# TensorE issues in written order until attention ends; thresholds move from ScalarE to VectorE

## The chip, the cores and the metric

The kernel runs on one core of a Trainium2 chip. The metric is the device time of one execution in microseconds (us). A core has five engines that run side by side, each working through its own queue in the order fixed when the program is built: TensorE (PE in the profile; its weight loads are PEld), VectorE (DVE), ScalarE (ACT), GpSimd (POOL) and SyncE (SP), which here issues the DMAs. An instruction that waits for another engine holds up all that stands behind it in its queue.

## What is computed

Attention with a threshold, then two feed-forward blocks, for 4 batches of 576 tokens with 8 heads of 64:

```python
scores = scale * np.matmul(q, k.transpose(0, 1, 3, 2))
thresh = np.max(scores, axis=-1, keepdims=True) - tau
scores = np.where(scores >= thresh, scores, -1000000000.0)
scores = scores - np.max(scores, axis=-1, keepdims=True)
attn = np.exp(scores)
attn = attn / (np.sum(attn, axis=-1, keepdims=True) + 1e-09)
x = np.matmul(attn, v)          # then heads side by side: 2304 x 512
...
h = (x @ w1) * (x @ w2) @ w3    # 1024 wide
x = h @ w_out                   # 2304 x 512
...
h = x @ w_in                    # 2048 wide
return np.maximum(0.01 * h, h) @ w_out2
```

## The kernel before, in words

**Steps and units.** Two heads (a pair) are worked on together. The 576 query rows of a pair are cut into group 0 (rows 0 to 255) and group 1 (rows 256 to 575). A pair and a group make a *unit* (32 units); per batch the four units of group 0 come first and then the four of group 1. A unit of group 0 has two *steps*, each with 128 rows of both heads (a double step); a unit of group 1 has one step in which the last 64 rows of both heads share one tile (c is None; a single step) and then two double steps. That gives 80 steps (`STEPS`, L33); the main loop (L450) goes over them.

**One step.** `scores` (L210) computes the scores of the next step n+1 on PE into the PSUM tile `sc`, of which there is one only, so that the scores of step n+1 wait for the mask of step n. Then, for each head, VectorE takes the negated maximum (L232), ScalarE makes the threshold from it (L233) and the exponential (L234). `mask` (L239) at the start of step n multiplies the exponential by "score is at or over the threshold" and sums it, on VectorE (L248). `transposes` (L254) turns the masked tile on PE, five 128 x 128 blocks per head, into `tp` (one buffer) and `tq`; ScalarE and VectorE copy them to `HH` and `tl` (L270 to L284). One step after the last of a unit, `weighted` (L288) computes v^T e on PE (L298, 20 matmul instructions) with a copy on ScalarE; two steps after it, `normalise` (L321) brings the reciprocals of the sums across with 2 to 4 PE instructions (L326, L328), multiplies by them on VectorE and splits the result in two parts on ScalarE and GpSimd.

**Filler.** Between these, PE does feed-forward work, the *filler*: for each batch and group, once its four units are normalised, the generator `gated` (L372) yields 24 pieces of 12 matmuls: 16 pieces psab (L385; products with w1 and w2, two per tile of w12) and 8 pieces psh (L404; the product with the folded weight w3 w_out). Filler made of group 0 runs beside the units of group 1 (256 columns per matmul), filler made of group 1 beside the next group 0 (320 columns). At each step `rate` times the weight of the step (1 or 2) pieces are due, half of them written ahead of the transposes and half behind (L462 to L465). In the first batch the folded weight itself is computed on PE instead (`fold_weights`, L357; L365, 8 blocks of 16 instructions). Filler, fold, v^T e and reciprocals share two PSUM buffers (`ps_w`, tag `w`).

**Weights.** They arrive as 64-bit words and are decoded in halves (`stream`, L108): two ScalarE passes (L150, L152), a shift on VectorE (L153), and an addition on GpSimd (L156); for the w12 and later weights a cast on ScalarE (L158), an addition on GpSimd (L159) and a subtraction on GpSimd or VectorE by turns (L161). `load_halves` (L431) is called at the end of each step; 24 halves serve the folding, 16 more the filler's w12.

**What sets the order.** A scheduler orders each engine's queue when the program is built, by a model of the timing and by priority, which falls in the order of writing. `ahead_of(60)` raises the priority of the scores' matmuls by 60 places, `ahead_of(20)` that of the transposes and of the late items (v^T e, normalising). SP alone keeps the written order (`manual_schedule`, L421) until the first batch's group 1 is through, and the decoding's ScalarE passes keep theirs. After attention (L499) the rest of the filler runs, and then the last feed-forward block (`up`, `down`).

Of the kernel before, what the change touches and what calls it, by code (L numbers as in the profile page):

```python
# [17 lines left out]
P = 128  # L18
# [21 lines left out]
def attention_gated_ffn(ctx: ExitStack, tc: tile.TileContext, qkv, tau, w3t, wout, w12, w2, out):  # L40
# [10 lines left out]

    @contextmanager
    def ahead_of(count):

        before = tc.cur_priority
        tc.cur_priority = start = before - count
        yield
        tc.cur_priority = before + (tc.cur_priority - start)
# [151 lines left out]
    def scores(n):  # L210
# [6 lines left out]
        with ahead_of(60):  # L217
            for half in range(2):
                ks = slice(half * HS, half * HS + HS)
                for a in heads:  # L220
                    if c is None:
                        nc.tensor.matmul(sc[:, a, half, :HS], qz[u % 2], qk[:, ks], start=True, stop=True)  # L222
                    else:
                        r = slice(a * D, a * D + D)
                        o = S + Q0[c] - GROUPS[g][0]
                        nc.tensor.matmul(sc[:, a, half, :HS], qk[r, o:o + P], qk[r, ks], start=True, stop=True)  # L226
        e = apool.tile([P, 2, S], F32, tag="e", name="e", bufs=2)
        ths = []
        for a in heads:
            nm = apool.tile([P, 1], F32, tag="nm", name="nm", bufs=4)  # L230
            th = apool.tile([P, 1], F32, tag="th", name="th", bufs=4)
            nc.vector.tensor_reduce(out=nm, in_=sc[:, a, :, :HS], op=ALU.max, axis=AX.XY, negate=True)  # L232
            nc.scalar.activation(th, nm, AF.Identity, bias=cb, scale=-1.0)  # L233
            nc.scalar.activation(  # L234
                e[:, a].rearrange("p (a b) -> p a b", a=2), sc[:, a, :, :HS], AF.Exp, bias=nm)
            ths.append(th)
# [17 lines left out]
    def transposes(n):  # L254
# [10 lines left out]
        if c is None:  # L265
            tp = ps_a.tile([P, 4, P], F32, tag="tp", name="tp")
            for kc in range(4):
# [4 lines left out]
                tail[D:, :, :D], tq[D:, 0].rearrange("p (a w) -> p a w", a=2))  # L272
            return
# [10 lines left out]
        nc.scalar.copy(tail[D:, :, o:o + P], tq[D:])  # L284
# [72 lines left out]
    def fold_weights():  # L357

        for i in range(KF):
# [4 lines left out]
            for j in range(KF):  # L364
                nc.tensor.matmul(  # L365
                    ps, w3_t[i][:, j * P:j * P + P], wo_t[j // 2][:, (j % 2) * 512:(j % 2) * 512 + 512],
                    start=(j == 0), stop=(j == KF - 1))
            nc.scalar.copy(wt[:, 0, i % 2], ps)
# [50 lines left out]

    in_order = ExitStack()  # L420
# [8 lines left out]
    halves_in = [0]  # L429

    def load_halves(k):  # L431
        for _ in range(k):
            if next(loads, 0) != 0:
                halves_in[0] += 1
                if 10 <= halves_in[0] <= 24 and halves_in[0] % 2 == 0:
                    next(folding)
# [5 lines left out]

    folding = fold_weights()
    scores(0)
    late = {}
    halves = 0.0
    filler = iter(())
    queue = []
    rate, due = 2.0, 0.0
    for n in range(NS):  # L450
        pair, g, c = STEPS[n]
        u = units.index((pair, g))
        weight = 1 if c is None else 2
        mask(n)
        if STEPS[(n + 1) % NS][:2] != (pair, g):
# [6 lines left out]
        run(filler, k // 2)  # L462
        with ahead_of(20):
            transposes(n)
        run(filler, k - k // 2)  # L465
        if STEPS[(n + 1) % NS][:2] != (pair, g):
            late.setdefault(n + 1, []).append(lambda pair=pair, g=g: weighted(pair, g))
            reciprocals(pair, g)
            late.setdefault(n + 2, []).append(lambda pair=pair, g=g: normalise(pair, g))
            if pair % 4 == 3:  # L470
                queue.append((n + 2, pair // 4, g))
        with ahead_of(20):
            for item in late.pop(n, []):
                item()
        if n == 0 or STEPS[n - 1][:2] != (pair, g):
            load_unit(u + 2)
        halves += 1.2 * weight
        load_halves(int(halves))
        halves -= int(halves)
        if queue and queue[0][0] == n:  # L480
            _, b, gg = queue.pop(0)
            while halves_in[0] < 24:
                load_halves(1)
            for _ in filler:
# [11 lines left out]
    for n in sorted(late):  # L496
        for item in late[n]:
            item()
# [138 lines left out]
```

## Time and profile before

| | us |
|---|---|
| Time, median of 3 runs | 1186.98 |
| lowest and highest of the runs | 1185.36, 1188.83 |
| the profiled execution's own time | 1189.11 |
| its span, first to last instruction | 1187.3 |
| mean granted TensorE clock, share of full speed | 0.968 |

The profile is of a single execution. Busy time of an engine counts the union of its instructions; matmuls are pipelined, so one of them is listed longer than the distance to the next start. The granted clock is a share of 2.4 GHz; its levels are 1.2 and 2.4 GHz.

### The profile page before, as it was taken

To read this page: it belongs to the slowest core of one execution; us is meant where nothing else is said; L and a number is where in the kernel's file an instruction comes from. 1 tells how busy PE (TensorE), PEld (TensorE's weight loads), DVE (VectorE), ACT (ScalarE), POOL (GpSimd) and SP (SyncE) were. 2 spreads that over 40 slices of the span, in tenths; PEclk is the share of its full clock that TensorE was granted. 3 is DMA by queue.
4 is the path that set the end of the run, shared out by engine and by line. 5 is a ranking of instruction groups with operands and counts; after the bars stand their busy time and mean duration, and the time that the engine had idled before them with its cause. 6 is when DMAs were issued, how large, how long until landed. Compare 5 with 4: busy or idle time off the path is not lost.

```text
span 1187.3 us, 16135 instructions
## 1 busy us (share of the span) xinstructions
PE 1099.6 (93%) x6288; PEld 864.6 (73%) x6288; DVE 471.5 (40%) x911; ACT 503.7 (42%) x1035; POOL 262.3 (22%) x288
## 2 busy tenths in 40 slices
PE   4799888999979998889998887999999999999998
PEld 2344466888857887667886665986788888888887
DVE  4554556444444544444544353336521121111111
ACT  4654666444443544334443344337732222222232
POOL 2322465111111111110210113547730010000000
PEclk9899989999989999889999888999999999999999
DMA  8542235211111112102111002226520010010000
GB/s 267 180 142 89 87 107 151 59 55 49 39 41 44 53 39 62 30 26 70 38 55 38 12 1 97 82 94 200 173 71 1 1 63 1 1 45 1 1 36 18
DMA packets 35099, 77.58 MB, mean 65 GB/s; under 512 B 4560, under 2 KB 19408, under 8 KB 32976
## 3 DMA queue, kind: packets, MB, share of 16 engines
q1 hardware_dynamic: 34880, 76.56, 20.6%
q8 instruction: 49, 0.80, 0.3%
q14 instruction: 26, 0.21, 0.1%
q10 hardware_dynamic: 144, 0.00, 0.0%
HBM read 67.11 MB, written 9.44 MB: 64 GB/s over the span
## 4 chain that ended last, share of the span: by engine, by line
PE 80%; ACT 8%; DVE 5%; issue 3%; DMA 2%; POOL 2%; SPq 0%; ACTq 0%; DVEq 0%; POOLq 0%
PE psab L385 17%; PE ps L552 15%; PE po L574 15%; PE psh L404 8%; PE av L298 7%; PE sc L226 6%; PE tp L278 5%; PE ps L365 3%; ACT e L234 2%; PE sc L222 2%; DVE nm L232 2%; ACT t L150 1%; DVE t L153 1%; ACT lw L152 1%; DVE e L248 1%
## 5 line engine op out<-in xcount | busy, mean ns | idle before, releaser
L385 PE MATMUL psab<-x,w 128*128 128x256 f32 (+1 forms) x1536 | 240.4, 308 | 10.0 <-ACT w L158 3.6
L385 PEld LDWEIGHTS psab<-x,w 128*128 128x128 f32 x1536 | 215.6, 195 | 33.9 <-issue 14.0
L552 PE MATMUL ps<-h,w 128*128 128x512 f32 (+1 forms) x960 | 215.7, 370 | 1.5 <-ACT w L158 1.2
L574 PE MATMUL po<-w,gg 128*128 128x512 f32 x864 | 213.6, 392 | 1.8 <-ACT gg L559 1.8
L552 PEld LDWEIGHTS ps<-h,w 128*128 128x128 f32 x960 | 169.0, 188 | 37.2 <-ACT w L158 2.5
L574 PEld LDWEIGHTS po<-w,gg 128*128 128x128 f32 x864 | 159.3, 188 | 37.8 <-ACT gg L559 3.0
L232 DVE TENSOR_REDUCE nm<-sc 128x1 f32<-128x576 f32 x144 | 108.8, 756 | 195.6 <-PE sc L226 135.3
L560 DVE TENSOR_TENSOR gg<-gf,gg 128x512 fp32r<-128x512 f32 (+1 forms) x80 | 61.2, 764 | 269.4 <-ACT gg L559 267.8
L557 ACT ACTIVATE gf<-ps 128x512 f32<-128x512 f32 (+1 forms) x80 | 44.2, 554 | 226.5 <-PE ps L552 226.5
L278 PE MATMUL tp<-ident,e 128*128 128x128 f32 x512 | 89.0, 301 | 53.7 <-DVE e L248 49.0
L248 DVE SCALAR_TENSOR_TENSOR e<-sc,th,e 128x576 f32<-128x576 f32 x144 | 112.5, 815 | 56.3 <-ACT e L234 56.0
L278 PEld LDWEIGHTS tp<-ident,e 128*128 128x128 f32 x512 | 64.8, 153 | 72.7 <-issue 57.8
L404 PE MATMUL psh<-gt,w 128*128 128x256 f32 (+1 forms) x768 | 112.8, 301 | 0.5 <-ACT xs L301 0.5
L404 PEld LDWEIGHTS psh<-gt,w 128*128 128x128 f32 x768 | 104.2, 190 | 4.1 <-issue 1.9
L234 ACT ACTIVATE e<-sc,nm 128x576 f32<-128x576 f32 x144 | 105.4, 732 | 1.0
L396 POOL TENSOR_TENSOR gt<-at,gt 128x256 fp32r<-128x256 f32 (+1 forms) x64 | 52.4, 819 | 189.8 <-ACT gt L395 189.8
L226 PE MATMUL sc<-qk 64*128 64x288 f32 x512 | 85.4, 448 | 6.4 <-DVE qk L201 6.0
L233 ACT ACTIVATE th<-nm,cb 128x1 f32<-128x1 f32 x144 | 42.4, 295 | 99.0 <-DVE nm L232 98.9
L298 PE MATMUL av<-HH,vv 128*64 128x256 f32 (+1 forms) x512 | 72.5, 424 | 0.1
L159 POOL TENSOR_TENSOR lw<-t,lw 128x512 int32<-128x512 int32 x48 | 64.8, 1356 | 27.6 <-ACT lw L152 15.8
L226 PEld LDWEIGHTS sc<-qk 64*128 64x128 f32 x512 | 46.5, 194 | 28.8 <-issue 12.3
L153 DVE TENSOR_SCALAR t<-t 128x512 int32<-128x512 int32 x72 | 50.0, 697 | 39.7 <-ACT t L150 39.4
(70 smaller groups left out, 968.3 us busy)
## 6 DMA issues: line engine op xcount, KB each, us to landing
st<-in_w SPq DMA_DIRECT2D x40, 512.0 KB, 4.5
vv<-in_qkv SPq DMA_DIRECT2D x64, 160.0 KB, 2.3
raw<-in_w3t SPq DMA_DIRECT2D x8, 1024.0 KB, 6.9
qk<-in_qkv SPq DMA_DIRECT2D x32, 208.0 KB, 3.6
qk<-in_qkv SPq DMA_DIRECT2D x32, 144.0 KB, 2.9
out<-os SPq DMA_DIRECT2D x18, 256.0 KB, 2.2
raw<-in_wout SPq DMA_DIRECT2D x4, 1024.0 KB, 10.3
raw<-in_w SPq DMA_DIRECT2D x4, 1024.0 KB, 7.3
```

What stands on the lines that cost most here:

```text
L153: nc.vector.tensor_scalar(out=t, in0=t, scalar1=3, scalar2=None, op0=ALU.logical_shift_left)
L159: nc.gpsimd.tensor_tensor(out=lw, in0=t, in1=lw, op=ALU.add)
L226: nc.tensor.matmul(sc[:, a, half, :HS], qk[r, o:o + P], qk[r, ks], start=True, stop=True)
L232: nc.vector.tensor_reduce(out=nm, in_=sc[:, a, :, :HS], op=ALU.max, axis=AX.XY, negate=True)
L234: nc.scalar.activation(e[:, a].rearrange("p (a b) -> p a b", a=2), sc[:, a, :, :HS], AF.Exp, bias=nm)
L248: nc.vector.scalar_tensor_tensor(out=ev, in0=sc[:, a, :, :HS], scalar=th, in1=ev, op0=ALU.is_ge, op1=ALU.mult, accum_out=stat[key][:, o:o ...
L278: nc.tensor.transpose(tp[:, kc], e[:, a, kc * P:kc * P + P], ident)
L298: nc.tensor.matmul(av[a * D:a * D + D, :gw], vv[:, a, kc], rhs, start=(i == 0), stop=(i == NK - 1))
L385: nc.tensor.matmul(ps[:, :gw], w12_t[i][:, a, mat * 512 + kk * P:mat * 512 + kk * P + P], xt[kk][:, c, :gw], start=(m == 0), stop=(m == 11))
L404: nc.tensor.matmul(ps[:, :gw], w34_t[i // 2][:, a, i % 2, o * P:o * P + P], gt[i][:, c, :gw], start=(m == 0), stop=(m == 23))
L552: nc.tensor.matmul(ps[:, :tw], w2_t[j][:, a, kk * P:kk * P + P], h3_t[ci][:, c, kk, :tw], start=(m == 0), stop=(m == 11))
L574: nc.tensor.matmul(po_t[t], gg[:, c, t * P:t * P + P], w2_t[j][:, a, 512:], start=(j == 0 and (a, c) == PASSES[0]), stop=(j == KF2 - 1 and ...
```

## The change

- PE keeps the written order from the start to the end of attention; the priorities (`ahead_of`) are gone.
- The written order of a step is new: scores of the next step; a third of the filler due; v^T e of the previous unit, if due; the transposes of the first head; another third; the transposes of the second head; the reciprocals of the unit before, if due; the last third. Where there is one piece it goes to the first place, two go to the first and second.
- The fold is cut into 16 pieces of 8 matmul instructions. Each of the three filler places takes one, provided that the halves it needs had been decoded before the step began; what is left is written when the first filler is made.
- Half of a step's decoding is written after the first third of filler, the rest at the end, now behind the loads of the unit after next.
- The threshold is made by a VectorE instruction in place of one on ScalarE.

```diff
--- before.py
+++ after.py
...
     def f(ap):
         return ap.bitcast(F32)
-
-    @contextmanager
-    def ahead_of(count):
-
-        before = tc.cur_priority
-        tc.cur_priority = start = before - count
-        yield
-        tc.cur_priority = before + (tc.cur_priority - start)
...
         heads = range(1 if c is None else 2)
         sc = ps_a.tile([P, 2, 2, 512], F32, tag="sc", name="sc")
-        with ahead_of(60):
-            for half in range(2):
...
+        for half in range(2):
+            ks = slice(half * HS, half * HS + HS)
...
             th = apool.tile([P, 1], F32, tag="th", name="th", bufs=4)
             nc.vector.tensor_reduce(out=nm, in_=sc[:, a, :, :HS], op=ALU.max, axis=AX.XY, negate=True)
-            nc.scalar.activation(th, nm, AF.Identity, bias=cb, scale=-1.0)
+            nc.vector.tensor_scalar(out=th, in0=nm, scalar1=-1.0, scalar2=cb, op0=ALU.mult, op1=ALU.add)
             nc.scalar.activation(
                 e[:, a].rearrange("p (a b) -> p a b", a=2), sc[:, a, :, :HS], AF.Exp, bias=nm)
             ths.append(th)
@@ -270,6 +261,7 @@
             nc.scalar.copy(HH[:, :, :, :D], tp.rearrange("p k (a w) -> p k a w", a=2))
             nc.vector.tensor_copy(
                 tail[D:, :, :D], tq[D:, 0].rearrange("p (a w) -> p a w", a=2))
+            yield
             return
         o = Q0[c] - GROUPS[g][0]
         for a in range(2):
@@ -281,7 +273,9 @@
             else:
                 nc.scalar.copy(HH[:, :, a, o:o + P], tp)
             nc.tensor.transpose(tq[:, a], e[:, a, S - P:], ident)
-        nc.scalar.copy(tail[D:, :, o:o + P], tq[D:])
+            if a:
+                nc.scalar.copy(tail[D:, :, o:o + P], tq[D:])
+            yield
 
     xs_t, x_t, rb_t = {}, {}, {}
 
@@ -365,6 +359,8 @@
                 nc.tensor.matmul(
                     ps, w3_t[i][:, j * P:j * P + P], wo_t[j // 2][:, (j % 2) * 512:(j % 2) * 512 + 512],
                     start=(j == 0), stop=(j == KF - 1))
+                if j == 3:
+                    yield
             nc.scalar.copy(wt[:, 0, i % 2], ps)
             nc.vector.tensor_tensor(out=wt[:, 1, i % 2], in0=ps, in1=f(wt[:, 0, i % 2]), op=ALU.subtract)
             yield
@@ -417,6 +413,8 @@
             yield from gn
 
 
+    pe_order = ExitStack()
+    pe_order.enter_context(tc.manual_schedule(engines={mybir.EngineType.PE}))
     in_order = ExitStack()
     in_order.enter_context(tc.manual_schedule(engines={mybir.EngineType.SP}))
     load_tau()
@@ -427,60 +425,83 @@
     issue()
     scale_unit(0)
     halves_in = [0]
+    folded = [0]
 
     def load_halves(k):
         for _ in range(k):
             if next(loads, 0) != 0:
                 halves_in[0] += 1
-                if 10 <= halves_in[0] <= 24 and halves_in[0] % 2 == 0:
-                    next(folding)
 
     def run(gen, k):
         for _ in range(k):
             if next(gen, 0) == 0:
                 return
 
+    def fold_some(most, halves):
+
+        while most and folded[0] < 2 * KF and 8 + 2 * (folded[0] // 2) + 2 <= halves:
+            next(folding, 0)
+            folded[0] += 1
+            most -= 1
+
     folding = fold_weights()
     scores(0)
-    late = {}
-    halves = 0.0
+    weigh, norm = [], []
+    due_halves = 0.0
     filler = iter(())
     queue = []
-    rate, due = 2.0, 0.0
+    rate, due = 0.0, 0.0
     for n in range(NS):
         pair, g, c = STEPS[n]
         u = units.index((pair, g))
         weight = 1 if c is None else 2
+        last_of_unit = STEPS[(n + 1) % NS][:2] != (pair, g)
+        decoded = halves_in[0]
         mask(n)
-        if STEPS[(n + 1) % NS][:2] != (pair, g):
+        if last_of_unit:
             scale_unit(u + 1)
         if n + 1 < NS:
             scores(n + 1)
         due += rate * weight
         k = int(due)
         due -= k
-        run(filler, k // 2)
-        with ahead_of(20):
-            transposes(n)
-        run(filler, k - k // 2)
-        if STEPS[(n + 1) % NS][:2] != (pair, g):
-            late.setdefault(n + 1, []).append(lambda pair=pair, g=g: weighted(pair, g))
+        parts = [(k + 2) // 3, (k + 1) // 3, k // 3]
+        due_halves += 1.2 * weight
+        kh = int(due_halves)
+        due_halves -= kh
+
+        def fill(i):
+            run(filler, parts[i])
+            fold_some(1, decoded)
+
+        fill(0)
+        load_halves(kh // 2)
+        if weigh:
+            weighted(*weigh.pop())
+        pieces = transposes(n)
+        next(pieces)
+        fill(1)
+        for _ in pieces:
+            pass
+        if norm:
+            normalise(*norm.pop())
+        if last_of_unit:
             reciprocals(pair, g)
-            late.setdefault(n + 2, []).append(lambda pair=pair, g=g: normalise(pair, g))
-            if pair % 4 == 3:
-                queue.append((n + 2, pair // 4, g))
-        with ahead_of(20):
-            for item in late.pop(n, []):
-                item()
+            weigh.append((pair, g))
+        elif u and STEPS[n - 1][:2] != (pair, g):
+            norm.append(units[u - 1])
+        fill(2)
         if n == 0 or STEPS[n - 1][:2] != (pair, g):
             load_unit(u + 2)
-        halves += 1.2 * weight
-        load_halves(int(halves))
-        halves -= int(halves)
+        load_halves(kh - kh // 2)
+        if last_of_unit and pair % 4 == 3:
+            queue.append((n + 2, pair // 4, g))
         if queue and queue[0][0] == n:
             _, b, gg = queue.pop(0)
-            while halves_in[0] < 24:
+            while halves_in[0] < 26:
                 load_halves(1)
+            fold_some(2 * KF, 24)
+            next(folding, 0)
             for _ in filler:
                 pass
             if (b, gg) == (0, 0):
@@ -493,9 +514,10 @@
                 in_order.close()
             filler = gated(b, gg)
             rate, due = (1.22, 1.55)[gg], 0.0
-    for n in sorted(late):
-        for item in late[n]:
-            item()
+    weighted(*weigh.pop())
+    run(filler, 2)
+    normalise(B * 4 - 1, 1)
+    pe_order.close()
     s_att.close()
 
 
```

## Rows read from the trace of the kernel before

**Rows 1.** The page, part 1: busy us, share of the span, instructions of each engine
```profile
PE 1099.6 (93%) x6288; PEld 864.6 (73%) x6288; DVE 471.5 (40%) x911; ACT 503.7 (42%) x1035; POOL 262.3 (22%) x288
```

**Rows 2.** Busy time by stretch: us, PE, PEld, DVE, ACT, POOL busy (instructions), PEclk, DMA share, GB/s
```profile
0.00:60.20 60.20, 35.45 (x162) 19.99 (x162) 32.96 (x74) 31.14 (x61) 16.20 (x20) 0.94 0.68 220
60.20:132.00 71.80, 65.77 (x250) 32.52 (x250) 35.67 (x72) 36.32 (x73) 22.09 (x24) 1.00 0.30 96
132.00:227.20 95.20, 85.00 (x540) 63.23 (x538) 54.53 (x109) 59.52 (x126) 44.11 (x46) 0.93 0.40 121
227.20:300.60 73.40, 72.52 (x509) 61.26 (x507) 35.02 (x75) 31.97 (x73) 12.92 (x18) 1.00 0.17 51
300.60:396.90 96.30, 88.22 (x622) 70.59 (x621) 46.84 (x103) 42.81 (x97) 16.17 (x28) 0.95 0.15 44
470.40:566.70 96.30, 84.03 (x577) 65.17 (x576) 46.30 (x101) 41.14 (x92) 14.75 (x26) 0.93 0.15 42
639.90:735.00 95.10, 78.69 (x502) 58.75 (x501) 39.85 (x86) 38.04 (x84) 16.51 (x27) 0.86 0.06 17
```

**Rows 3.** Groups by line, PE, 0 to 745 us: busy us, mean ns, idle before, releasers
```profile
L278 PE MATMUL tp<-ident,e 128*128 128x128 f32 x512 | 89.0, 301 | 53.7 <-DVE e L248 49.0 <-ACT HH L282 3.7 <-ACT HH L270 0.8
...
L365 PE MATMUL ps<-wo,w 128*128 128x512 f32 x128 | 58.5, 601 | 6.3 <-POOL w L156 6.2
```

**Rows 4.** Timeline of all engines, 684.7 to 697.3: start us, us, instructions [idle before, releaser]
```profile
685.65 4.57 PE L385 MATMUL psab<-x,w 128*128 128x256 f32 x36 [0.18 <-DVE xs L329]
...
688.00 0.81 DVE L248 SCALAR_TENSOR_TENSOR e<-sc,th,e 128x576 f32<-128x576 f32 x1
...
690.06 0.60 PE L278 MATMUL tp<-ident,e 128*128 128x128 f32 x4
...
690.70 1.24 PE L226 MATMUL sc<-qk 64*128 64x288 f32 x8
...
691.99 0.76 DVE L232 TENSOR_REDUCE nm<-sc 128x1 f32<-128x576 f32 x1 [2.67 <-PE sc L226]
...
692.78 0.29 ACT L233 ACTIVATE th<-nm,cb 128x1 f32<-128x1 f32 x1 [0.17 <-DVE nm L232]
693.09 0.74 ACT L234 ACTIVATE e<-sc,nm 128x576 f32<-128x576 f32 x1
693.86 0.76 DVE L232 TENSOR_REDUCE nm<-sc 128x1 f32<-128x576 f32 x1 [0.49 <-ACT e L234]
...
694.85 0.72 ACT L234 ACTIVATE e<-sc,nm 128x576 f32<-128x576 f32 x1
695.61 0.82 DVE L248 SCALAR_TENSOR_TENSOR e<-sc,th,e 128x576 f32<-128x576 f32 x1 [0.99 <-ACT e L234]
...
696.58 1.09 PE L278 MATMUL tp<-ident,e 128*128 128x128 f32 x4 [3.95 <-DVE e L248]
```

**Rows 5.** Timeline of PE, 676 to 706
```profile
677.79 2.37 PE L298 MATMUL av<-HH,vv 128*64 128x320 f32 x16
680.10 1.69 PE L385 MATMUL psab<-x,w 128*128 128x256 f32 x12
681.72 1.24 PE L226 MATMUL sc<-qk 64*128 64x288 f32 x8
```

**Rows 6.** Single source lines: count, ns min/median/max, first and last start
```profile
L309 DVE TENSOR_SCALAR rr<-stat x32: 156/161/1256, 24.0 to 721.0; 128x4 f32<-128x4 f32 x16, 128x5 f32<-128x5 f32 x16
...
L153 DVE TENSOR_SCALAR t<-t x72: 409/471/2622, 18.2 to 862.0; 128x512 int32<-128x512 int32 x72
...
L152 ACT ACTIVATE lw<-st x40: 643/663/695, 171.6 to 861.9; 128x512 int32<-128x512 uint32 x40
...
L158 ACT CAST w<-t x48: 600/619/646, 133.1 to 862.5; 128x512 fp32r<-128x512 f32 x48
...
L161 POOL TENSOR_TENSOR w<-lw,w x24: 1268/1357/1738, 134.2 to 862.2; 128x512 fp32r<-128x512 f32 x24
```

**Rows 7.** The page, part 6, DMA issues: count, KB each, median us to landing
```profile
qk<-in_qkv SPq DMA_DIRECT2D x32, 208.0 KB, 3.6
```

More of the change, by code (lines that the diff above doesn't have):

```diff
@@ L1 @@
-from contextlib import ExitStack, contextmanager
+from contextlib import ExitStack
 import concourse.bass as bass
@@ L216, in scores @@
         sc = ps_a.tile([P, 2, 2, 512], F32, tag="sc", name="sc")
-        with ahead_of(60):
-            for half in range(2):
[L219 to L226, printed above, removed]
+        for half in range(2):
+            ks = slice(half * HS, half * HS + HS)
+            for a in heads:
+                if c is None:
+                    nc.tensor.matmul(sc[:, a, half, :HS], qz[u % 2], qk[:, ks], start=True, stop=True)
+                else:
+                    r = slice(a * D, a * D + D)
+                    o = S + Q0[c] - GROUPS[g][0]
+                    nc.tensor.matmul(sc[:, a, half, :HS], qk[r, o:o + P], qk[r, ks], start=True, stop=True)
         e = apool.tile([P, 2, S], F32, tag="e", name="e", bufs=2)
```

## The prediction

> **What bounds it now.** I read the page's busy line first. TensorE (PE) is busy for 1099.6 of 1187.3 us [rows 1], no other engine for half of the span, so the time can only fall where PE stands still or runs slowly. Second, the table of stretches [rows 2], cut where the kind of filler changes: PE's idle time there is length minus PE busy. The stretch 227.2 to 300.6, in which units of group 0 run, is idle for 0.9 us of 73.4: nothing is to be had there, nor in the two later stretches of its kind. The three stretches of group 1 (from 300.6, 470.4 and 639.9) are idle for 8.1, 12.3 and 16.4 us, and their granted clock is 0.95, 0.93 and 0.86. Since the clock has two levels, 1.2 and 2.4 GHz, a share of 2 x (1 - mean) was at the lower one: 10, 13 and 27 us. In the first batch (three stretches up to 227.2) PE idles 24.8, 6.0 and 10.2 us.
>
> Third, the groups by line with what ended the idle time before them: of PE's idle time up to 740 us, 49.0 us is transposes (L278) waiting for the mask (L248) [rows 3]. Fourth, the timeline of one such wait [rows 4]. PE runs 36 psab matmuls in one go until 690.1 while the mask that the next scores need had ended at 688.8 (second mask row: 688.00 + 0.81); the scores start at 690.70. From there VectorE and ScalarE work strictly in turn: maximum 691.99, exp 693.09, maximum 693.86, exp 694.85, then two masks of 0.8 us from 695.61, the last of which ends near 697.2. PE has used up its filler and stands for 3.95 us; the four transposes after it take 1.09 us where they took 0.60 at 690.06, so the lower clock is paid as well. The work is there, but it is done at the wrong moment. What is late is not an engine but the scores, behind filler.
>
> **The change, part by part.**
>
> 1. *Written order on PE, group 1.* A unit has three steps (one single, two double). Its PE work, from starts in one undisturbed part [rows 5]: a piece of 12 psab or psh matmuls 1.6 us (680.10 to 681.72), double scores 1.2 us, v^T e 2.3 us for 16 matmuls (677.79 to 680.10), so 2.9 us for its 20. Five transposes are 0.64 us (690.06 to 690.70, [rows 4]), single scores 1.1 and the reciprocals' four matmuls 0.5 us, as much as four transposes. One unit: 2 x 1.2 + 1.1 + 6.1 x 1.6 + 5 x 0.64 + 2.9 + 0.5 = 20 us; four units 80 us, against 96.3 us per stretch. The idle time and the slow clock account for this: idle 8.1 + 12.3 + 16.4 = 36.8 us, and at the lower clock about 50 us, of which some 7 us are idle inside it; busy time at half clock gives back half, 21 us. Together 58 us to be had at most.
>
> What does written order leave of it? I walk one unit. The wait is now at the scores, for the mask of the step before; behind it on PE's queue stand filler, v^T e and the transposes, all of it. The chain from the end of double scores to the end of the second mask was 691.9 to 697.2 = 5.3 us [rows 4]; with part 2 it is 4.8 us, for a single step about 2.6. Cover between two scores: after the single step's scores one piece and five plus five transposes, with a piece between: 1.6 + 0.64 + 1.6 + 0.64 = 4.5 us over 2.6, no wait. After the first double scores one piece, v^T e and five transposes: 1.6 + 2.9 + 0.6 = 5.1 us over 4.8: it just fits, and any copy that gets between (0.4 to 0.7 us on either engine) shows. After the second, three pieces, ten transposes and 0.5: 6.6 us over 4.8. I charge 0.7 us for the middle one and 0.5 us for filler that waits for one of the two PSUM buffers which filler, v^T e and reciprocals share: the piece behind the reciprocals' matmuls has only 0.64 + 0.5 us for its buffer's evacuation. 1.2 us x 12 units = 14 us; bounds 0 and 12 x 4 = 48 us (as much as now is lost).
>
> 2. *Thresholds on VectorE.* Removes 144 activations of 0.29 us from ScalarE, where each stood ahead of the exp (692.78 ahead of 693.09, [rows 4]). Adds 144 small operations to VectorE; the nearest row, the small tensor_scalar of L309, has a median of 161 ns and would run beside the exp (0.74 us), since the next maximum starts only when that exp has ended. So 0.2 to 0.3 us off the chain, twice per double step. Where PE is the bound this is worth nothing; where nothing covers the chain (the first five steps) 5 x 0.4 = 2 us. The cost could show if the small operation grows: L309 has one case of 1256 ns, and the tensor_scalar of L153 goes from 409 to 2622 ns (both [rows 6]). I take 161 ns as the median and no cost.
> The Trainium skill ("SBUF — State Buffer", Who interferes with whom) says that VectorE's tensor_scalar may need a port pair that GpSimd holds for a whole instruction, the later one being blocked. By that rule a threshold that meets a GpSimd addition of 1.3 us ends up to 0.7 us after the exp; with GpSimd busy for 46% of the third stretch [rows 2] and 36 thresholds in the first batch, 36 x 0.46 x 0.35 on average, the sum would be about 6 us worse. The spread of L153 agrees with the rule; no run here shows it for so small an operand.
>
> 3. *First batch, folding (L365).* Now cut into 16 pieces of 8 matmuls (58.5 us in all, 3.7 us each [rows 3]) and one per filler place, held until the decoded halves stand one step back. Nothing of it comes before step 5, so two pieces that now run before 58 us are left for later: their cover for the first steps is lost, 7 us worse (bounds 4 and 7.4). The 6.2 us of waits for decoded weights (same row) have better lead, but the queue is now blocked behind them: no change, bounds -4 and +6.
>
> 4. *First batch, gated filler (132 to 227.2).* To be had: 10.2 + 6.0 us idle and half of 13 us at the lower clock, 22 us. The filler's weights are decoded just ahead of use, and one half takes ScalarE two passes of 0.66 (L152, and L150 like it) and one of 0.62 (L158), VectorE 0.47 (L153), GpSimd 1.36 and for every other half as much again (L161, and L159 like it) [rows 6]: about 5 us end to end, each pass behind the other engines' other work. In written order scores, v^T e and transposes behind such a piece wait too. ScalarE is the fullest here (59.5 of 95.2 us); squeezed into 80 us of PE work it is at 74%. I charge 10 us for 16 tiles; bounds 0 and 16 x 3.9 = 62 (the whole 5.1 us less the 1.2 us of scores ahead of it).
>
> 5. *Group 0 in later batches.* 12 units; the stretch from 227.2 spends 73.4 us on its eight steps [rows 2], 9.2 us each, so some 8 us of cover stand over 4.8: no wait at the scores. The buffer after the reciprocals' matmuls can cost 0.25 us: 3 us.
>
> 6. *What is moved.* v^T e now goes ahead of the transposes instead of behind the last filler; the reciprocals' matmuls behind them, with their VectorE, ScalarE and GpSimd successors; nothing waits on these for a step. Half of the decoding (with the SP loads that each half issues) moves ahead of the next unit's q, k and v loads on SP. Those are asked for two units (some 20 us) ahead, so I cost it at nothing; without that cover it would be the 3.6 us of one such load [rows 7] per unit. The part behind 735 us keeps its 452 us.
>
> **Sum.** Gain 58 + 22 + 2 = 82; losses 14 + 7 + 10 + 3 = 34 plus 2 us at the end of attention, where no scores are left to overlap. Net 46 us. The profiled execution took 1189.1 us (span 1187.3), 2.1 us over the median of the runs; I take the 46 us off the median: 1141.
>
> **Rivals.**
> - *The wait moves from transposes to scores.* If copies or products that VectorE and ScalarE take in between lengthen the chain from 4.8 to 6.5 us or more, every group 1 unit loses about 1.3 us at the first and some at the second cover, and with the buffers 2.5 to 3 us. For: [rows 4] shows strict turns with no slack. Against: group 0 stretches do not wait at all. 12 x 1.5 more, and a third of that again in the first batch: some 25 us less gain, 1166.
> - *Nearly all is got back.* If the charges of parts 1, 4 and 5 (27 us) mostly do not arise, 1115.
> - *Slower: decoded weights block the queue.* Place: the first 192 psab matmuls. Today PE's order, although fixed, has other work ahead of late weights (6.2 us of waits at L365 in all). If each of the 16 tiles waits the whole 3.9 us, 62 us instead of 10; added stalls at the folding and the lower clock after each wait of this length take the rest. It decides from (46 + 10) / 16 = 3.5 us per tile with every other gain as above, and from 1.9 us if the first rival holds as well. Alone it gives 1193, with the clock about 1205. Against: halves are decoded a step's filler ahead, so half of the tiles have a lead.
> - *The order hardly differs.* PE's queue was already near written order, and times stay at 1187. Against: 36 psab matmuls in one go.
>
> **Chances.** Forecast 0.48, first rival 0.22, all got back 0.10, slower 0.13, no change 0.07. A change under 0.3% (3.6 us) can't be told from none here. Faster 0.80, same 0.07, slower 0.13. The forecast's own range is 1120 to 1158 (half to double its charges); with the first rival's upper end and most of the second it is 1116 to 1184.
>
> **What would show it.** Right: PE's wait for L248 at transposes gone and at the scores (L222, L226) under 15 us in all; idle time in the group 1 stretches under 5 us each and the clock at 1.00 from 230 us on; attention ending near 690 us; exp starting within 0.1 us of the maximum. Wrong: waits at the scores of 1 us and more in each unit (first rival); waits of psab for L158 or L161 above 25 us, with the clock below 0.9 before 230 us (slower); small VectorE rows for the threshold of 0.5 us and more on the chain.

## Result, and the profile after

The changed kernel takes 1118.0 us (median of 4 runs, 1116.9 to 1118.6), the kernel before 1187.9 beside it: a ratio of 0.941, interval 0.939 to 0.943. It is faster by 70 us where 46 were forecast; 1118.0 lies at the lower end of the range, 1116 to 1184, and just below the narrower range that the prediction gave for its own forecast, 1120 to 1158.

Part 1 of the page, to be set beside [rows 1]:

```profile
PE 1062.5 (95%) x6288; PEld 856.3 (77%) x6288; DVE 499.6 (45%) x1055; ACT 475.2 (43%) x891; POOL 262.6 (24%) x288
```

The same 6288 matmuls; TensorE idles for 1116.2 - 1062.5 = 53.7 us of its span instead of 87.7, and is busy for 37 us less. Part of this is the clock: the mean granted clock rose from 0.968 to 0.989, so by 2 x (1 - mean) the time at 1.2 GHz fell from about 76 to 25 us. If work takes twice as long there (four transposes took 1.09 us against 0.60 [rows 4]), this explains at most half of the 51 us, 26 of the 37; the rest stays open. 34 us less idle and 37 us less busy are the 71 us of the span.

The table of stretches of the changed kernel, cut at the same steps as [rows 2] (length, PE, PEld, DVE, ACT, POOL busy with instructions, PEclk, DMA share, GB/s):

```profile
0.00:58.00 58.00, 34.61 (x163) 20.27 (x164) 37.82 (x95) 30.87 (x53) 16.72 (x20) 0.91 0.72 229
58.00:125.30 67.30, 66.16 (x234) 32.35 (x233) 32.28 (x67) 32.43 (x58) 25.89 (x27) 1.00 0.38 124
125.30:212.10 86.80, 75.99 (x540) 61.22 (x539) 61.45 (x132) 56.75 (x107) 39.83 (x42) 0.96 0.34 106
212.10:282.70 70.60, 68.28 (x480) 57.76 (x479) 37.43 (x89) 28.71 (x56) 12.96 (x18) 0.98 0.22 60
282.70:364.50 81.80, 80.54 (x608) 67.10 (x607) 50.42 (x123) 36.98 (x72) 14.24 (x26) 1.00 0.19 55
364.50:435.00 70.50, 68.18 (x478) 58.12 (x477) 37.39 (x89) 28.81 (x56) 12.95 (x18) 0.98 0.16 43
435.00:517.20 82.20, 80.64 (x610) 67.15 (x609) 50.42 (x123) 36.98 (x72) 14.23 (x26) 1.00 0.18 54
517.20:586.20 69.00, 66.68 (x480) 56.71 (x479) 37.39 (x89) 28.69 (x56) 12.97 (x18) 1.00 0.15 44
586.20:665.00 78.80, 77.30 (x584) 64.77 (x584) 42.51 (x103) 33.76 (x68) 14.41 (x27) 1.00 0.07 23
```

The group 1 stretches took 96.3, 96.3 and 95.1 us and take 81.8, 82.2 and 78.8 now: 45 us. Their idle time is 1.3, 1.6 and 1.5 us, their clock 1.00. Up to the change of filler (132.0, now 125.3) 6.7 us went, in the rest of the first batch 95.2 - 86.8 = 8.4. The three group 0 stretches give the other 10 us, but these are lent: some 30 filler matmuls in each (480 instructions against 509 in the first) are left to the stretch behind, about 4 us each at 1.6 us for 12 [rows 5], 12 us in all. The group 1 stretches do that work too: they hold 101 matmuls more than before (608 + 610 + 584 against 622 + 577 + 502), and are shorter by 45 us all the same.

The chain of waits of TensorE, 0 to 680 us (engine, tile and line, what it waited for: us in total, times, longest):

```profile
PE sc L217 <- DVE e L239: 20.0, 11, 4.9
PE sc L217 <- DVE qk L193: 8.3, 2, 6.0
PE tp L270 <- ACT HH L274: 7.3, 10, 1.6
PE sc L213 <- POOL qz L197: 5.8, 8, 2.1
PE psab L381 <- POOL w L153: 1.8, 3, 0.8
```

The 49.0 us in which transposes waited for the mask [rows 3] are gone. Scores wait for it instead, 20.0 us in all, of which 10.0 lie in the first 58 us, where there is no filler.

A unit of group 1 in the timeline of the changed kernel, to be set beside [rows 4] (start, length, instruction, [idle before it]):

```profile
606.03 0.81 DVE L239 SCALAR_TENSOR_TENSOR e<-sc,th,e 128x576 f32<-128x576 f32 x1
...
607.20 1.24 PE L217 MATMUL sc<-qk 64*128 64x288 f32 x8
...
608.49 0.76 DVE L223 TENSOR_REDUCE nm<-sc 128x1 f32<-128x576 f32 x1 [0.89 <-PE sc L217]
609.28 0.74 ACT L225 ACTIVATE e<-sc,nm 128x576 f32<-128x576 f32 x1 [1.44 <-DVE nm L223]
609.28 0.21 DVE L224 TENSOR_SCALAR th<-nm,cb 128x1 f32<-128x1 f32 x1
...
610.15 0.42 DVE L389 TENSOR_TENSOR at<-psab,at 128x256 f32<-128x256 f32 x1 [0.66 <-PE psab L381]
...
610.50 0.75 DVE L223 TENSOR_REDUCE nm<-sc 128x1 f32<-128x576 f32 x1
...
611.32 0.75 ACT L225 ACTIVATE e<-sc,nm 128x576 f32<-128x576 f32 x1
...
612.10 0.82 DVE L239 SCALAR_TENSOR_TENSOR e<-sc,th,e 128x576 f32<-128x576 f32 x1 [0.61 <-ACT e L225]
...
612.73 1.67 PE L381 MATMUL psab<-x,w 128*128 128x256 f32 x12
...
612.85 0.81 DVE L239 SCALAR_TENSOR_TENSOR e<-sc,th,e 128x576 f32<-128x576 f32 x1
...
613.58 0.38 DVE L193 TENSOR_SCALAR qk<-qk,scl 128x320 f32<-128x320 f32 x1
613.88 0.68 DVE L272 COPY HH<-tp 128x512 f32<-128x512 f32 x1
614.03 0.52 POOL L197 COPY qz<-qk 64x64 f32<-64x64 f32 x2 [1.79 <-DVE qk L193]
...
614.61 1.24 PE L213 MATMUL sc<-qk,qz 128*128 128x288 f32 x4 [0.21 <-POOL qz L197]
```

Read it as a race. From the end of the double scores (608.44) the chain goes maximum, exp, a product of the filler, maximum, exp, two masks, the scaling of the next unit's queries and the copies that place them: ready at 614.55, after 6.1 us. TensorE's cover ends with the last piece of filler at 614.40, after 6.0 us. They are level, and TensorE stands for 0.21 us. The profile of before does not show that they are level, since the wait stood elsewhere, though the scaling's length can be read there (0.37 us, the median of its L201). A race that is level means that anything which lengthens the chain shows in full.

### The profile page after: what moved, and what is told of

Read it like the earlier page. It is cut to its first block, busy times and chain, and to the rows that moved or that the text cites. A ratio compares the mean times of both kernels' runs of the same rounds, so it can differ in the third digit from the quotient of the medians.

```text
span 1116.2 us, 16066 instructions
## 1 busy us (share of the span) xinstructions
PE 1062.5 (95%) x6288; PEld 856.3 (77%) x6288; DVE 499.6 (45%) x1055; ACT 475.2 (43%) x891; POOL 262.6 (24%) x288
## 4 chain that ended last, share of the span: by engine, by line
PE 77%; issue 8%; ACT 5%; DVE 4%; POOL 2%; DMA 2%; SPq 0%; ACTq 0%; DVEq 0%; POOLq 0%
PE po L596 16%; PE ps L574 16%; PE psab L381 14%; PE psh L400 9%; PE av L292 6%; PE sc L217 6%; PE ps L359 5%; PE tp L270 4%; PE sc L213 2%; DVE e L239 2%; ACT t L142 1%; DMA st<-in_w 1%; ACT e L225 1%; POOL gt L392 1%; ACT lw L144 1%
## 5 line engine op out<-in xcount | busy, mean ns | idle before, releaser
L400 PE MATMUL psh<-gt,w 128*128 128x256 f32 (+1 forms) x768 | 115.2, 301 | 0.6 <-ACT ht L407 0.5
L217 PE MATMUL sc<-qk 64*128 64x288 f32 x512 | 85.3, 454 | 28.4 <-DVE e L239 20.0
L270 PE MATMUL tp<-ident,e 128*128 128x128 f32 x512 | 80.1, 280 | 7.3 <-ACT HH L274 7.3
L270 PEld LDWEIGHTS tp<-ident,e 128*128 128x128 f32 x512 | 60.6, 143 | 21.7 <-issue 11.6
L151 POOL TENSOR_TENSOR lw<-t,lw 128x512 int32<-128x512 int32 x48 | 64.9, 1357 | 39.4 <-ACT lw L144 24.5
L292 PE MATMUL av<-HH,vv 128*64 128x256 f32 (+1 forms) x512 | 69.5, 415 | 0.0
L551 POOL TENSOR_TENSOR h<-hr,h 128x1024 fp32r<-128x1024 f32 (+1 forms) x10 | 23.8, 2381 | 188.1 <-DVE h L550 188.1
```

What stands on the lines that cost most here:

```text
L151: nc.gpsimd.tensor_tensor(out=lw, in0=t, in1=lw, op=ALU.add)
L270: nc.tensor.transpose(tp[:, kc], e[:, a, kc * P:kc * P + P], ident)
L292: nc.tensor.matmul(av[a * D:a * D + D, :gw], vv[:, a, kc], rhs, start=(i == 0), stop=(i == NK - 1))
L400: nc.tensor.matmul(ps[:, :gw], w34_t[i // 2][:, a, i % 2, o * P:o * P + P], gt[i][:, c, :gw], start=(m == 0), stop=(m == 23))
```

## The experiments

Theory: the new order pays off only as long as the chain through the score tile stays within the cover, so the edits are worth little alone, and the last tenths off the chain are worth much. Rival: the written order is the gain, the rest detail. The theory came out of the first four runs; their own expectations still held the order to be the likelier cause.

**The threshold back on ScalarE, all else as changed.**

```diff
-nc.vector.tensor_scalar(out=th, in0=nm, scalar1=-1.0, scalar2=cb, op0=ALU.mult, op1=ALU.add)
+nc.scalar.activation(th, nm, AF.Identity, bias=cb, scale=-1.0)
```

> The changed kernel with the threshold back on ScalarE, all else as changed. If the order on TensorE made the gain (my reading): the chain from scores to mask gets about 0.45 us longer per double step, which shows only at the start (five steps, 2 us) and at the tightest place of each group 1 unit (0.1 to 0.3 us): 1121 us, between 1118 and 1127. If the shorter chain made the gain (rival): over 1140 us, with 1 us or more of wait at the scores in every group 1 unit.

1143.4 us, ratio 0.962 (0.959 to 0.966), in the range of the expectation's rival (over 1140): the edit is worth 25 us. TensorE's order is the same in both kernels. VectorE's is not: the scheduler still orders that queue, and 35 of its 770 other instructions stand at another place in this run. The same place of a unit in its timeline:

```profile
632.21 1.24 PE L217 MATMUL sc<-qk 64*128 64x288 f32 x8 [0.23 <-DVE e L239]
...
634.28 0.30 ACT L224 ACTIVATE th<-nm,cb 128x1 f32<-128x1 f32 x1 [1.74 <-DVE nm L223]
634.48 0.72 ACT L225 ACTIVATE e<-sc,nm 128x576 f32<-128x576 f32 x1
...
636.34 0.29 ACT L224 ACTIVATE th<-nm,cb 128x1 f32<-128x1 f32 x1
...
636.53 0.73 ACT L225 ACTIVATE e<-sc,nm 128x576 f32<-128x576 f32 x1
...
637.52 0.69 DVE L272 COPY HH<-tp 128x512 f32<-128x512 f32 x1 [1.27 <-PE tp L270]
...
638.13 0.81 DVE L239 SCALAR_TENSOR_TENSOR e<-sc,th,e 128x576 f32<-128x576 f32 x1
...
640.63 1.24 PE L213 MATMUL sc<-qk,qz 128*128 128x288 f32 x4 [1.22 <-POOL qz L197]
```

Each threshold delays its exp by 0.2 us, and the second exp ends 0.2 us later behind the scores than in the changed kernel (3.8 us against 3.6). The first mask starts 1.0 us later behind them (4.7 against 3.7): VectorE's queue has a copy of HH (0.69 us) ahead of it, which in the changed kernel stands behind the masks (613.88). From the end of the scores, 633.45, to the placed queries, 640.58, it is 7.1 us instead of 6.1, and TensorE stands for 1.22 us. So at this place most of the 1.0 us comes from VectorE's order, which changed with the edit, and not from the 0.2 us; how the 25 us as a whole split between the two was not separated. Both lengthen the same chain. The three group 1 stretches (88.2, 88.2 and 81.1 us) hold some 15 us of the 25; the rest lies in the first batch and the group 0 stretches. A unit takes 20.1 us (starts of scores 5.0, 6.6 and 8.4 apart) where the changed kernel's takes 18.7 (5.0, 6.3, 7.4). In the first five steps the difference is 2.3 us.

**The threshold on VectorE alone, in the kernel before** (there the old line stands at L233).

```diff
-nc.scalar.activation(th, nm, AF.Identity, bias=cb, scale=-1.0)
+nc.vector.tensor_scalar(out=th, in0=nm, scalar1=-1.0, scalar2=cb, op0=ALU.mult, op1=ALU.add)
```

> The kernel before with the threshold on VectorE and nothing else changed. If the order made the gain: the long waits of transposes for the mask each shorten by about 0.45 us, with some of the slow clock behind them: 1180 us, between 1172 and 1187. If the shorter chain made it (rival): under 1160 us and those waits nearly gone.

1155.1 us, ratio 0.973 (0.970 to 0.976): over 30 us faster by this one line, again the time of the rival (under 1160), though the waits are not nearly gone. Waits of that kernel:

```profile
PE tp L278 <- DVE e L248: 30.2, 9, 6.3
```

The waits for the mask fell from 49.0 to 30.2 us. The scheduler also placed TensorE's work differently, so how much is the chain and how much the new order stays open for this run.

**The written order alone, in the kernel before.** The v^T e had to be written ahead of the transposes, since there is one HH buffer.

```diff
+pe_order = ExitStack()
+pe_order.enter_context(tc.manual_schedule(engines={mybir.EngineType.PE}))
...
+            if n in av_at:
+                weighted(*av_at.pop(n))
             transposes(n)
```

> The kernel before with TensorE held to its written order and v^T e written ahead of the transposes; filler in two halves around both heads' transposes, whole fold blocks, threshold on ScalarE as before. If holding the order is what matters and the finer spreading a second, smaller part (my reading): the scores come right after the mask, but the second head's transposes wait 0.6 to 0.7 us for the first head's copy out of the single buffer in 64 double steps: 1150 us, between 1130 and 1165. If holding alone does it all (rival): under 1128. If only the new placing does (rival): over 1175.

1226.9 us, ratio 1.032 (1.029 to 1.036): slower by 38 us. Of the three expectations only the open-ended last one (over 1175) holds it, and none forecast a slower kernel. Waits:

```profile
PE tp L278 <- ACT HH L282: 40.4, 64, 1.7
PE sc L226 <- DVE e L248: 38.6, 21, 5.6
PE ps L365 <- POOL w L156: 22.4, 7, 6.3
```

The written order with the old writing puts the wait for the mask at the scores (the first rival's picture), waits at every second head's transposes, and lets whole folds block the queue.

**The new writing without the hold on TensorE's order.**

```diff
-    pe_order = ExitStack()
-    pe_order.enter_context(tc.manual_schedule(engines={mybir.EngineType.PE}))
...
-    pe_order.close()
```

> The changed kernel without the hold: new writing order, threshold on VectorE, but TensorE's queue again ordered by the scheduler, without the former priorities. If the hold matters: filler runs ahead of the scores again, waits of several us for the mask and stretches at the lower clock come back: 1170 us, between 1145 and 1195. If the new writing alone does it (rival): under 1128.

1146.2 us, ratio 0.964 (0.961 to 0.967), so the hold is worth 28 us here. The wait is back at the transposes:

```profile
PE tp L270 <- DVE e L239: 37.4, 16, 4.2
```

**Both heads' transposes together, a third of the filler behind them.**

```diff
-        next(pieces)
-        fill(1)
         for _ in pieces:
             pass
+        fill(1)
```

> The changed kernel with the transposes of both heads one after the other and the second third of filler behind them. If the filler between the heads hides the copy out of the single buffer (my reading): 0.6 us of wait in each of 64 double steps, 38 us, of which some takes the place of waits at the scores: 1145 us, between 1130 and 1160, with waits of tp for HH near 40 us. If only the order at large matters (rival): 1118, at most 1123.

1170.0 us, ratio 0.987 (0.984 to 0.989): the place of this filler is worth 52 us, twice what I expected.

```profile
PE tp L270 <- ACT HH L274: 48.1, 64, 2.5
```

There is one PSUM tile for transposed blocks. In 64 places the second head's transposes wait 0.75 us on average for the copy of the first head's; with filler between them it was 7.3 us in all.

**The scaling of the next unit's queries ahead of the masks.**

```diff
-        mask(n)
         if last_of_unit:
             scale_unit(u + 1)
+        mask(n)
```

> The changed kernel with the scaling of the next unit's q traced ahead of the mask of the unit's last step instead of behind it. If the scores of a unit's first step wait not for the mask alone but for scaling and the qz copy queued behind it (my new reading, about 0.9 us on the chain once per unit): waits for qz and qk gone, 1112 us, between 1108 and 1116. If the mask alone is what is waited for (my forecast's reading): 1118, at least 1116.5.

1156.3 us, ratio 0.976 (0.973 to 0.979), a miss: 38 us slower than the changed kernel. The timeline shows why:

```profile
646.56 0.68 DVE L272 COPY HH<-tp 128x512 f32<-128x512 f32 x1
647.16 0.47 DVE L323 TENSOR_TENSOR xs<-xs,bc 128x320 f32<-128x320 f32 x1
...
647.63 0.41 DVE L389 TENSOR_TENSOR at<-psab,at 128x256 f32<-128x256 f32 x1
...
647.96 0.38 DVE L193 TENSOR_SCALAR qk<-qk,scl 128x320 f32<-128x320 f32 x1
...
649.01 0.52 POOL L197 COPY qz<-qk 64x64 f32<-64x64 f32 x2
...
649.58 1.24 PE L213 MATMUL sc<-qk,qz 128*128 128x288 f32 x4 [2.21 <-POOL qz L197]
```

The scaling did not move forward: it stands behind the masks, a copy and two products, and then GpSimd was busy. The scores wait 2.21 us for it. That the scaling lies on the chain is shown by this; that moving it helps is not. With the threshold back on ScalarE as well:

> The run with the threshold on ScalarE, and the scaling ahead of the mask as in the run before. If the threshold's 25 us come from a chain without slack, longest where scaling and qz end it: most of the loss in group 1 units goes: 1128 us, between 1121 and 1134. If they come from ScalarE's load or its queue order elsewhere (rival): 1138 or more.

1182.4 us, ratio 0.997 (0.995 to 0.998), a miss as well (1128 expected, 1138 or more by the rival): the two losses add up (1118.0 + 25 + 38 = 1181).

**The scaling in an earlier step.** So that nothing of this kind stands behind the last masks:

```diff
-        if last_of_unit:
+        if c == 2 or (c == 0 and u) or (c == 1 and not u):
             scale_unit(u + 1)
```

> The change whole, with the scaling of the next unit's queries (and the two copies that place them into the zeroed block) called behind the masks of an earlier step of the unit instead of its last step: group 1 in its middle step, group 0 in its first. Theory (the scaling and the copies behind the last masks stand between the masks and the next scores, 0.38 and 0.52 us each): the waits of the scores for the placed queries, 5.8 us in 8 times in the changed kernel, are gone, with some of the lower clock that followed the two of over 2 us: about 1112 us (1108 to 1116), and a score's first wait in group 1 is for the mask alone. Rival (they are covered in any case; the run with the scaling ahead of the masks was slower for its own place, behind the filler's last product): 1118 us as the changed kernel, with the waits passed on to the masks.

1111.7 us, ratio 0.936 (0.935 to 0.938), as the theory said. No score waits for placed queries any more; a group 1 unit takes 18.4 us (5.0, 6.3, 7.0).

**Scores of the two heads in two PSUM tiles**, so that the maximum of the second head need not wait for the exp of the first.

```diff
-        sc = ps_a.tile([P, 2, 2, 512], F32, tag="sc", name="sc")
+        sc = [ps_a.tile([P, 2, 512], F32, tag=f"sc{a}", name="sc") for a in heads]
```

(and `sc[:, a, ...]` written `sc[a][:, ...]`)

> The changed kernel with the scores of the two heads in two PSUM tiles of two banks each instead of one tile of four. If the strict turns of VectorE and ScalarE come from sharing one tile (my reading): the second maximum runs beside the first exponential, the chain falls from 4.8 to about 3.3 us, the waits at the scores mostly go, and the first five steps get 1 to 1.5 us shorter each: 1106 us, between 1099 and 1112. If the turns have another cause (rival): 1118, at least 1116.

1093.3 us, ratio 0.922 (0.920 to 0.924): 25 us better than the changed kernel, where 6 to 19 were expected. Timeline of a double step:

```profile
602.68 1.24 PE L217 MATMUL sc<-qk 64*128 64x288 f32 x8
...
603.95 1.42 DVE L223 TENSOR_REDUCE nm<-sc 128x1 f32<-128x576 f32 x2 [0.87 <-PE sc L217]
...
604.75 1.41 ACT L225 ACTIVATE e<-sc,nm 128x576 f32<-128x576 f32 x2 [1.43 <-DVE nm L223]
...
606.68 0.81 DVE L239 SCALAR_TENSOR_TENSOR e<-sc,th,e 128x576 f32<-128x576 f32 x1
```

Both maxima run back to back (x2 in 1.42 us), both exps as well; from the end of the scores, 603.92, to the end of the last mask, 607.49, it is 3.6 us where it was 5.2. The waits of the scores for the mask are gone, but for one of 2.6 us behind a threshold.

**Two tiles, with the threshold on ScalarE.** The sharpest test of the theory: with slack in the chain, the same line should cost nothing.

> The change with the scores of the two heads in two PSUM tiles, and the thresholds on ScalarE as before. Theory (what the move of the thresholds was worth, 25.3 us beside the shared tile, was the length of a chain without slack from one step's scores through maximum, exponential and masks to the next step's scores; with two tiles the heads overlap and the chain has slack): the thresholds cost little now, about 1098 us (1094 to 1105) against 1093 with them on VectorE. Rival (the thresholds hold up ScalarE itself, or the order of the copies on VectorE, whatever the tiles): about 20 to 25 us over the 1093, so 1113 to 1118.

1095.4 us, ratio 0.923 (0.921 to 0.924): 2.0 us over the 1093.3, where the same edit cost 25 with the shared tile. VectorE's queue changes here too (30 of 770 instructions), and under this slack neither that nor the 0.2 us per threshold costs much.

**Two tiles alone, in the kernel before.**

> The kernel before (TensorE's order left to the scheduler, thresholds on ScalarE, whole folds, filler in halves) with one edit: the scores of the two heads in two PSUM tiles. Theory (the wait of 49.0 us of the transposes for the masks is the same chain, and any shortening of it is paid back even without the written order): about 1145 us (1125 to 1162), like the thresholds alone, which gave 1155; the waits for the masks well below 30 us. Rival (without the written order the scheduler spends the slack elsewhere, since it places TensorE's work by its own model): 1175 us or more.

1166.7 us, ratio 0.983 (0.981 to 0.984), worse than the theory's 1145 (1125 to 1162) and nearer to the rival's 1175. The rival had the cause in outline (the scheduler places TensorE's work by its own model), but not what it was. Part 1 of its page, and its group of double scores by line:

```profile
PE 1126.2 (97%) x6288; PEld 883.4 (76%) x6288; DVE 477.5 (41%) x911; ACT 498.6 (43%) x1035; POOL 262.4 (23%) x288
```

```profile
L226 PE MATMUL sc<-qk 64*128 64x288 f32 x512 | 140.5, 458 | 10.5 <-DVE qk L201 6.5 <-DVE e L248 4.0
```

The waits did go: idle time fell from 87.7 to 38.8 us, and the waits for the mask to about 11. But TensorE was busy for 27 us longer with the same matmuls: the 512 double scores took 140.5 us where they take 85.3 in the changed kernel. One step of each in the timelines, first this kernel's, then the changed kernel's:

```profile
616.17 1.23 PE L226 MATMUL sc<-qk 64*128 64x288 f32 x4
```

```profile
600.87 1.24 PE L217 MATMUL sc<-qk 64*128 64x288 f32 x8
```

Four products of 64 rows in the time of eight. Written head by head in turn, two products start 7 ns apart and run side by side; once each head had its own tile, the scheduler no longer kept them together. By the starts in the traces, 76 of the 256 pairs begin within 10 ns here and 252 in the kernel before. So 55 us of scores took back most of what the waits and the clock gave. With the shared tile the scheduler keeps the pairs without the hold (254 in the run without it); with two tiles and the hold there are 246. Once there are two tiles, the written order is thus needed for a second thing, to keep the pairs.

**The best of it together:** two tiles, the earlier scaling, and the gated filler of group 0 (written beside group 1's steps) spread a little thinner, over all of them.

```diff
-            rate, due = (1.22, 1.55)[gg], 0.0
+            rate, due = (24 / 21, 1.55)[gg], 0.0
```

> The change with three edits together: scores of the two heads in two PSUM tiles; the scaling of the next unit's queries in an earlier step; and the filler of the first group-0 pass of each later batch spread at 24/21 products per weight instead of 1.22, so that it lasts over its 21 weights. Theory: with two tiles (1093) little idle is left before the tail, so the two further edits can give back only the remaining 12 us of waits for the copy of HH and part of the clock: 1090 us (1086 to 1093). Rival (the filler spread thinner leaves the copies' waits longer): 1096 us.

1087.8 us (1085.7 to 1088.2), ratio 0.916 (0.914 to 0.918), within the theory's range: faster than both kernels, by 30 us than the changed one.

```profile
PE 1053.0 (97%) x6288; PEld 851.4 (78%) x6288; DVE 492.1 (45%) x1055; ACT 470.8 (43%) x891; POOL 264.4 (24%) x288
```

How much of the 5.6 us over two tiles alone is the scaling and how much the spreading was not separated.

## Why the prediction was right, and where it was wrong

The direction, the place and the mechanism of the change were right; one term was far too small, and some others came out near for other reasons than those given.

- *Part 2, thresholds: the step that failed.* The prediction said "Where PE is the bound this is worth nothing", and took 2 us. It is worth 25 with all else in place, the moves in VectorE's queue that it brings included. The durations were right: the exp follows the maximum at once (609.28 behind 608.49 + 0.76), 0.2 us earlier per head, and the first five steps gave the 2 us (2.3 measured). What was wrong is the cover. Part 1 set "6.6 over 4.8" for the third step of a unit. The masks end 4.7 to 5.2 us behind the scores, as said, but for a unit's first scores the chain goes on through scaling (0.38) and copies (0.52), which the prediction never counted, and the cover was 6.0: no slack at all, so TensorE was not the bound there. With two tiles, which give slack, the same line cost 2.0 us. Without this term the net forecast is 44 us, and the run with the threshold on ScalarE shows 45 (by its ratio, 0.962). That the rest agrees as a sum is partly luck: its charges were made for a chain that part 2 had already shortened to 4.8 us, and they did not come at the places named (parts 1, 3 and 4 below).
- *Part 1, the order of group 1.* Charged 14 us, that is 4.7 per stretch; idle time there is 1.3 to 1.6 us. The charge of 1.2 us per unit is about what the run with the threshold on ScalarE shows (20.1 against 18.7 us), but it stood for the middle scores and the shared PSUM buffers, and that run waits for 0.23 us at the middle scores and 1.22 at the next unit's first; the interplay with part 2 was missed. The middle cover, "5.1 over 4.8", came out (602.11 to 607.20, masks done at 606.84).
- *Part 3, folding.* Charged 7 us with the wait for decoded weights unchanged; the stretch up to the change of filler is 6.7 us shorter, its idle time 24.5 us instead of 30.8. The sum had 1 us of gain there (2 of part 2 and 6.0 of idle time counted in part 4, less the 7), so the charge did not show. In pieces, the folding waits for weights no longer (6.2 us before).
- *Part 4, the first gated filler.* 12 us of net gain forecast, of which 6.0 are the idle time of the stretch ahead; 8.4 found in this one. They are not idle time won: 86.8 - 76.0 = 10.8 us stand idle where 10.2 did. The stretch of before still held 14 matmuls of the fold (6.2 us), which now lie ahead of it. The 10 us charged are about right in size, for another reason: decoded weights hold psab up for 1.8 us in all, while waits for placed queries take 4.2 us here and waits for the mask 3.1. For the first batch as a whole, parts 2 to 4 gave 22 + 2 - 7 - 10 = 7 us, and 15 were found. The slower rival (3.5 us on each of 16 tiles) did not come.
- *Part 5, group 0.* Charged 3 us in all; 2.3 us of idle time stand in each of the three stretches, 7 in all, where the one of before had 0.9 [rows 2]. Under-sized, but small.
- *The port rule.* The threshold took 214 ns where the prediction took 161 from the nearest row, with no spread (single line, changed kernel; count, ns min/median/max):

```profile
L224 DVE TENSOR_SCALAR th<-nm,cb x144: 200/214/217, 9.1 to 649.0; 128x1 f32<-128x1 f32 x144
```

  None of the 144 was held up, with GpSimd busy for 46% of the third stretch (39.8 of 86.8 us). 33 of them began while a GpSimd instruction was running, and took 213 to 216 ns. The Trainium skill ("SBUF — State Buffer", Who interferes with whom) says that a tensor_scalar can contend with GpSimd for a port pair, if its operands meet certain conditions. These rows show nothing of that for an operand of one column. The 6 us that the prediction estimated from it did not come.
- *The rivals.* "Nearly all is got back" gave 1115, nearest to the result, but its condition held for part 1 alone (4.3 us idle against 14 charged) and not for parts 4 and 5 (10.8 and 7 against 10 and 3), so that number is partly luck. The first rival points at what the kernel is without the threshold edit, waits at the scores and units of 20 us; that run waits about half as much per unit as the rival said, and takes 1143 and not 1166.
- *The range.* "1120 to 1158 (half to double its charges)" does not follow from the sum: with 36 us of losses, half and double give 1123 and 1177.
- *What was to show it.* Waits at the scores under 15 us: 20.0, wrong by what lies in the first 58 us. Idle time under 5 us in the group 1 stretches: yes. Clock 1.00 from 230 us on: 0.98 in two stretches. End of attention near 690: earlier, the last reciprocals' input starts at 652.3 where it was 721.0. Exp within 0.1 us of the maximum: yes.

## What to carry to other kernels

When an order is written by hand, measure every chain that must fit under a cover to its very end, up to the instruction that releases the next scores, and put the margin beside it: one small edit in the chain, with the moves in VectorE's queue that came with it, cost 2 us where the chain had margin and 25 where it had none. Look also which queues an edit reorders that you did not mean to touch. An edit that loses alone can be needed in company: the hold lost 38 us alone and was worth 28 beside the others. Before tuning a chain of turns, look whether two engines take turns only because they share a tile: two tiles gave 25 us more.

## What the runs showed that I had not expected

- Paired products of 64 rows: eight in 1.24 us when the two heads alternate, four in 1.23 when they don't; 55 us over 512 products. The Trainium skill ("TensorEngine Tiling (Array Packing)", Key Properties) says that different tiles of the array can run matmuls in parallel; the rows agree, and show that this hangs on the order in which the products are issued.
- Less idle time came with less busy time for the same matmuls, but at no fixed rate: 34 us with 37 in the change itself, 20 with 7 between the run with the threshold on ScalarE and the changed kernel. The granted clock is not all of it: with both heads' transposes together, 36 us more idle time came with 16 us more busy time at nearly the same mean clock (0.988 against 0.989). What the rest is stays open. In the kernel with two tiles the mean clock is 0.998.
